# A mixture-of-experts kernel: experts visited in four groups ahead of the tail, 40 visits instead of 48

## The chip, the cores and the metric

The kernel runs on one core of a Trainium2 chip. Its engines are TensorE (PE in the profile, its weight loads PEld), VectorE (DVE), ScalarE (ACT), GpSimd (POOL) and SyncE (SP, which here only issues DMAs). The metric is the device time of one execution in microseconds; less is better.

## The reference, cut to what matters

A causal convolution of 7 taps with softmaxed weights per head runs over x (8 x 2880 rows of 192). Its 23,040 output rows go through a two-level mixture of experts: the best of 4 groups, then the best of that group's 4 experts, one expert of 16 for each row.

```python
g_idx = np.argmax(x @ w_group, axis=1)
# for each group g, of its rows xg:
e_idx = np.argmax(xg @ w_expert[g], axis=1)
h = np.maximum(xg[mask_e] @ w1[g, e], 0.0)      # 192 -> 1024
ye = h @ w2[g, e]                               # 1024 -> 192
out[tok_idx] = combined[:, None] * ye           # combined: both softmax weights
```

The results are float32. With the inputs used, the experts get between 1252 and 1628 rows.

## The kernel before

**Routing.** The rows are cut into 18 units of 4, 8 or 12 blocks of 120 rows; the last twelve units have 12 blocks. A unit (`unit`) convolves its rows on TensorE (line 498), ScalarE copies them to SBUF (lines 503, 505), and they are stored to the DRAM table `xcd` (lines 507, 664) with each row's softmax weight. Units 0 to 11 make their logits in float32 from TensorE transposes (lines 519 to 597). Units 12 to 17 (`THIN` = 12 and above) cut their rows into 16-bit parts on ScalarE and VectorE (`parts_a`, `parts_b`, lines 550 to 560), transpose these with DMAs issued by SP (`cross`, line 564) and multiply them on TensorE (line 573). VectorE then picks the expert and counts positions (lines 631 to 712), TensorE and VectorE make a list of row numbers for each expert (lines 718 to 722), and GpSimd scatters it into the table `idtab` (line 724).

**Where a unit's rows lie.** `rows_of` gives a unit a buffer from `room_tile`: by turns one of two `xc` tiles or one of two halves of the tile `spare`. Units 12 to 17 always take `xc`, since their 16-bit parts (`cut_tile`) lie in thirds of `spare`.

**Expert work.** It goes through `plan`, a list of slots. A slot gathers a block of row numbers (`gather`, GpSimd indirect DMA, line 806), transposes it on TensorE (`turn`, lines 824 to 830), multiplies by w1 (`hidden`, line 857; `hidden_wide`, line 895), applies relu (ScalarE, line 862) and forms the remainder `hl` (VectorE, line 863), multiplies by w2 (`back`, lines 875, 879), scales (ScalarE, line 933), adds (VectorE, line 940) and scatters into `out` (`finish`, line 941). To keep float32 accuracy on the fast matmul format every operand is split into a high and a low part. The first slot of an expert's turn is a visit: `weights` loads w1 and w2 through SP (lines 741 to 746) and ScalarE and VectorE split them in four steps (lines 763 to 776), into `ah`, `al`, `bb` and `cw`. Later slots of the same visit reuse the weights.

**The stages of the plan.** Portion 0 starts when 5 units are routed: one slot of 256 rows for each of the 16 experts. Portion 1 needs 12 units: two slots for each. The tail needs all units: the rest of each expert, in pieces. `PIECES` lists 16 sizes, from the largest rest to the smallest, such as (256, 384, 256); an expert's rank by its rest picks its entry, and `ORDER` the order in which ranks are visited. Visits: 16 + 16 + 16 = 48.

**What sets the order.** One program writes all queues. While it writes the slots it calls `advance` sixteen times a slot, which lets the units step forward at `rate`: the units' remaining stages until each portion's need, over the slots until that portion starts less 5 (`MARGIN`); the largest of these counts. `open_slot(i)` is called two slots ahead of slot i: it loads weights, and gathers. When the unit that a portion needs is finished, `open_portion` is called at most four `open_slot` calls later (`HOLD`): it reads the row numbers from `idtab` into `idp` through SP and moves each expert's consumed count `cons` on (`consume`). A scheduler then orders each engine's instructions.

```python
rate[0] = max(
    [(stages_to(portions[q][0]) - done[0]) / (max(starts[q] - MARGIN - i, 1) * 2 * NF)
     for q in starts if q not in idps] + [0.0])
```

## Time and profile before

| | |
|---|---|
| three timed runs, us | 1108.94, 1109.41, 1112.72; median 1109.41 |
| the profiled execution | 1113.36 us, span of its instructions 1111.6 us |
| TensorE matmul busy | 1060.5 us, 95% |
| weight loads on TensorE | 1030.6 us, 93% |
| VectorE | 776.5 us, 70% |
| ScalarE | 685.1 us, 62% |
| GpSimd | 538.2 us, 48% |
| DMA | 161.15 MB, mean 145 GB/s |
| mean granted clock of TensorE | 0.979 |

The span runs from the first to the last instruction; the profiled execution is 1.8 us longer than its span. Busy shares are means over very different stages: the first 92 us hold routing alone, the expert slots with routing beside them go on to about 530 us, and then slots run alone. So the windows by stage tell more than the page. Matmuls overlap in the records, and their ends are modelled. An arrow in a row names what ended an engine's idle time, which stands behind it in us.

### The profile page before, as it was taken

The numbers are of one execution on the slowest core, as the hardware profiler recorded it, in microseconds if no ns is written. First come the engines' busy times: TensorE is split into PE (matmuls) and PEld (weight loads), VectorE is DVE, ScalarE is ACT, GpSimd is POOL, SyncE is SP. The second block draws the span as 40 slices with busy tenths as digits, with TensorE's granted clock in tenths as the row PEclk, the third lists the DMA queues.
The fourth block names the chain that finished last, engine by engine and source line by source line (L and its number), as shares of the span: only waits on it lengthen the run. The fifth ranks groups of instructions, "written<-read, shape, count | busy, mean of one in ns | idle before, by whom it ended". The sixth has DMA issues, their size and how long they took to land. (4 is left out here: it accounts for less than half of the span.)

```text
span 1111.6 us, 22636 instructions
## 1 busy us (share of the span) xinstructions
PE 1060.5 (95%) x7986; PEld 1030.6 (93%) x7986; DVE 776.5 (70%) x1815; ACT 685.1 (62%) x1512; POOL 538.2 (48%) x485
## 2 busy tenths in 40 slices
PE   6799999989898999999999999999999999999997
PEld 5778899978898999999999999999999999999997
DVE  3746977788897888798669666656665656665662
ACT  5555566667674767675656666666666655655653
POOL 2013423334555555555646565555645555565542
PEclk9987999989999999999999999999999999999999
DMA  8978668898999777694455453333332323343210
GB/s 205 242 188 229 171 184 212 201 235 201 250 226 201 176 194 165 162 206 121 131 110 143 105 158 92 105 94 96 90 102 66 97 77 105 115 120 100 62 38 23
DMA packets 205814, 161.15 MB, mean 145 GB/s; under 512 B 87183, under 2 KB 189590, under 8 KB 205694
## 3 DMA queue, kind: packets, MB, share of 16 engines
q1 hardware_dynamic: 139696, 105.50, 37.6%
q0 software_dynamic: 19360, 36.09, 12.2%
q10 hardware_dynamic: 46638, 18.07, 7.5%
q8 instruction: 63, 1.03, 0.4%
q14 instruction: 57, 0.47, 0.2%
HBM read 113.06 MB, written 36.47 MB: 135 GB/s over the span
## 5 line engine op out<-in xcount | busy, mean ns | idle before, releaser
L875 PE MATMUL po<-cw,hh 128*128 128x384 f32 x1040 | 325.7, 371 | 1.1 <-ACT ys L933 1.1
L857 PE MATMUL ph<-xa,ah 128*128 128x256 f32 x1040 | 290.7, 300 | 6.8 <-DVE hl L863 3.3
L862 ACT ACTIVATE hh<-ph 128x512 fp32r<-128x512 f32 x260 | 153.6, 596 | 191.7 <-PE ph L857 145.9
L879 PE MATMUL po<-cw,hl 128*128 128x192 f32 x1040 | 261.8, 252 | 0.0
L863 DVE SCALAR_TENSOR_TENSOR hl<-ph,hh 128x512 fp32r<-128x512 f32 x260 | 176.9, 686 | 103.0 <-ACT hh L862 85.2
L806 POOL DMA_INDIRECT xg<-xcd,idp x128 | 149.1, 1165 | 195.3 <-ACT ys L933 115.2
L806 POOL DMA_INDIRECT xg<-xcd,idpt x127 | 135.4, 1066 | 162.9 <-ACT ys L933 67.1
L857 PE MATMUL ph<-xb,bb 128*128 128x256 f32 x1040 | 211.3, 285 | 1.8 <-DVE bb L768 1.8
L857 PEld LDWEIGHTS ph<-xa,ah 128*128 128x128 f32 x1040 | 199.9, 192 | 11.6 <-DVE hl L863 5.0
L879 PEld LDWEIGHTS po<-cw,hl 128*128 128x128 f32 x1040 | 200.2, 193 | 1.7
L875 PEld LDWEIGHTS po<-cw,hh 128*128 128x128 f32 x1040 | 197.3, 190 | 3.5 <-ACT ys L933 1.7
L857 PEld LDWEIGHTS ph<-xb,bb 128*128 128x128 f32 x1040 | 163.6, 193 | 2.2 <-DVE bb L768 2.0
L857 PE MATMUL ph<-xa,al 128*128 128x256 f32 x520 | 149.4, 287 | 0.0
L941 POOL DMA_INDIRECT out<-ys,idp x96 | 124.8, 1300 | 46.5 <-DVE ys L940 19.5
L941 POOL DMA_INDIRECT out<-ys,idpt x91 | 103.7, 1140 | 54.3 <-DVE ys L940 23.2
L933 ACT ACTIVATE ys<-po,xg 128x384 f32<-128x384 f32 x168 | 93.4, 580 | 34.8 <-PE po L879 14.9
L895 PE MATMUL ph<-xa,ah 128*128 128x384 f32 (+1 forms) x304 | 100.7, 335 | 4.2 <-DVE xc L901 3.3
L857 PEld LDWEIGHTS ph<-xa,al 128*128 128x128 f32 x520 | 100.3, 193 | 2.4 <-issue 0.2
L776 DVE TENSOR_TENSOR cw<-raw,cw 128x768 fp32r<-128x768 f32 x96 | 91.5, 953 | 9.9 <-ACT cw L775 7.0
L840 ACT ACTIVATE xb<-pm 64x128 fp32r<-64x128 f32 (+2 forms) x342 | 94.8, 277 | 3.1
L940 DVE TENSOR_TENSOR ys<-ys 128x192 f32<-128x192 f32 x179 | 61.7, 357 | 31.3 <-ACT ys L933 24.8
L775 ACT ACTIVATE cw<-raw 128x768 fp32r<-128x768 f32 x96 | 80.5, 845 | 0.1
(259 smaller groups left out, 2003.7 us busy)
## 6 DMA issues: line engine op xcount, KB each, us to landing
raw<-in_moe_w SPq DMA_DIRECT2D x96, 384.0 KB
raw<-in_moe_w SPq DMA_DIRECT2D x48, 512.0 KB
raw<-in_moe_w SPq DMA_DIRECT2D x48, 256.0 KB
xin<-in_x SPq DMA_DIRECT2D x7, 1134.0 KB
xcd<-xc ACTq DMA_DIRECT2D x10, 742.5 KB
xin<-in_x SPq DMA_DIRECT2D x6, 1039.5 KB
xcd<-xcb ACTq DMA_DIRECT2D x13, 360.0 KB
xcd<-spare ACTq DMA_DIRECT2D x3, 742.5 KB
```

The lines of the kernel that those rows point to most:

```text
L775: pin(PINW, nc.scalar.activation(out=cw[:, fs, 0, :], in_=rc[k - 2], func=AF.Copy))
L776: eng.get(k, nc.vector).tensor_tensor(out=cw[:, fs, 1, :], in0=rc[k - 2], in1=cw[:, fs, 0, :].bitcast(F32), op=ALU.subtract,)
L806: ins = nc.gpsimd.indirect_dma_start(out=rows[0:n, to:to + size], out_offset=None, in_=xcd[0:known, :], in_offset=bass.IndirectOffsetOnAxi ...
L840: nc.scalar.activation(out=xb[h:h + D2, 0, c:c + k], in_=pb, func=AF.Copy)
L857: nc.tensor.matmul(out=hp[:, j], lhsT=wgt[:, fs], rhs=xx, start=i == 0, stop=i == len(ops) - 1)
L862: nc.scalar.activation(out=hh, in_=hp, func=AF.Relu)
L863: lows.append(nc.vector.scalar_tensor_tensor(out=hl, in0=hp, scalar=0.0, in1=hh.bitcast(F32), op0=ALU.max, op1=ALU.subtract,))
L875: nc.tensor.matmul(out=oo[t][:, 0:2 * D], lhsT=hh[:, j, ts], rhs=cw[:, f].rearrange("p a d -> p (a d)"), start=f == 0, stop=False,)
L879: nc.tensor.matmul(out=oo[t][:, 0:D], lhsT=hl[:, j, ts], rhs=cw[:, f, 0, :], start=False, stop=f == NF - 1,)
L895: nc.tensor.matmul(out=hp[:, 0:w], lhsT=wgt[:, fs], rhs=xx, start=i == 0, stop=i == len(ops) - 1)
L933: nc.scalar.activation(out=y, in_=oo[t][0:n, 0:2 * D], func=AF.Copy, scale=g)
L941: nc.gpsimd.indirect_dma_start(out=outviews[nscat[0] % len(outviews)], out_offset=bass.IndirectOffsetOnAxis(ap=ids[t].bitcast(U32), axis=0 ...
```

## The change

The three stages before the tail become five entries of `portions`, each with a range of experts: experts 0 to 7 get one slot each when 5 units are routed; experts 8 to 11 two slots each at 9 units; experts 12 to 15 three slots each at 12 units; experts 0 to 7 two more slots each at 13 units. Visits: 8 + 4 + 4 + 8 + 16 = 40. Experts 8 to 11 thus have taken 512 rows before the tail instead of 768, so `PIECES` grows by 1024 rows in sum, with a new `ORDER`. `open_portion` and `consume` work on a range of experts. Besides, `rows_of` gives units 9, 10 and 11 the tile `xc` too (`THIN - 3`), and the last unit waits 16 stages instead of 8 before it makes its list (`list_lag`).

```diff
--- before.py
+++ after.py
@@ -77,12 +77,12 @@
     LE = P // E
     XT = 64
     PIECES = (
-        [(256, 384, 256)] * 2 + [(256, 320, 256)] * 2 + [(384, 384)] + [(384, 320)] * 4 + [(384, 256)] * 3
-        + [(320, 256)] * 2 + [(256, 256)] * 2)
+        [(256, 384, 256)] * 3 + [(256, 320, 256)] * 3 + [(384, 384)] * 3 + [(384, 320)] * 4 + [(384, 256)] * 2
+        + [(320, 256)])
     CAPS = [sum(p) for p in PIECES]
-    MOST, WMAX = CAPS[0], max(w for p in PIECES for w in p)
+    MOST, WMAX = -(-CAPS[0] // P) * P, max(w for p in PIECES for w in p)
     NTAIL = len(PIECES)
-    ORDER = [5, 0, 6, 2, 7, 3, 8, 1, 4, 14, 9, 10, 11, 12, 13, 15]
+    ORDER = [9, 0, 10, 1, 11, 2, 12, 3, 6, 4, 7, 5, 8, 13, 14, 15]
     assert NTAIL == E and sorted(ORDER) == list(range(E)) and sorted(CAPS, reverse=True) == CAPS
     CAP = -(-(N + MOST) // 1024) * 1024
     DUMMY = E * CAP
@@ -102,7 +102,7 @@
 
     NEED = 5
     NEXT = 6
-    portions = [(NEED, 1), (NU - NEXT, 2), (NU, 0)]
+    portions = [(NEED, 0, 8, 1), (9, 8, 12, 2), (12, 12, E, 3), (13, 0, 8, 2), (NU, 0, E, 0)]
     LEAD = 8
     LAG = 3
     REST = 10
@@ -280,7 +280,7 @@
     def rows_of(u):
 
         if u not in packed:
-            xc = room_tile(0 if u >= THIN else None)
+            xc = room_tile(0 if u >= THIN - 3 else None)
             xb = pa4.tile([P, UB, D2], F32, name="xcb")
             off = 0
             for v in range(u, NEED):
@@ -304,7 +304,7 @@
     make_identity(nc, ident)
 
 
-    LIM = SLOT * sum(spe for _, spe in portions)
+    LIM = SLOT * max(sum(spe for _, lo, hi, spe in portions if lo <= e < hi) for e in range(E))
     FR = 2 * E
     fill = wraw.tile([P, F], F32, name="raw")[0:FR, 0:LIM // 2].bitcast(I32)
     nc.gpsimd.memset(fill, BIG)
@@ -467,6 +467,10 @@
         ga, gl, gb, _ = gaps(u)
         nq = units[u][1] // QB
         return 1 + APART * (nq - 1) + 4 + CROSS + 1 + gb if u >= THIN else ga + gl + gb + 3 * nq
+
+    def list_lag(u):
+
+        return 2 * LISTLAG if u == NU - 1 else LISTLAG
 
     def unit(u, pre=None):
         c0, nb = units[u]
@@ -711,7 +715,7 @@
         with nc.allow_low_precision(reason="whole numbers, summed in float32"):
             nc.vector.tensor_reduce(out=rowi, in_=rows, axis=AX.X, op=ALU.add)
         counted[0] = u + 1
-        for _ in range(LISTLAG if u >= NEED else LISTLAG0 if u < NEED - 1 else 0):
+        for _ in range(list_lag(u) if u >= NEED else LISTLAG0 if u < NEED - 1 else 0):
             yield
         pl = bank("l")
         for b in range(nb):
@@ -1093,13 +1097,14 @@
         yield tabt
 
 
-    def consume(quota):
+    def consume(quota, lo, hi):
         nc.vector.scalar_tensor_tensor(
-            out=cons, in0=cons, scalar=float(quota), in1=eold[:, counted[0], 0:E], op0=ALU.add, op1=ALU.min,
+            out=cons[:, lo:hi], in0=cons[:, lo:hi], scalar=float(quota), in1=eold[:, counted[0], lo:hi],
+            op0=ALU.add, op1=ALU.min,
         )
 
     def stages(u):
-        return 1 + 8 + turning(u) + gaps(u)[3] + 1 + (LISTLAG if u >= NEED else 0)
+        return 1 + 8 + turning(u) + gaps(u)[3] + 1 + (list_lag(u) if u >= NEED else 0)
 
     SKEW1 = 8
     LIVE1 = 4
@@ -1116,7 +1121,8 @@
     live = []
     done = [0]
     routed = [0, 0]
-    needs = {need: pi for pi, (need, _) in enumerate(portions)}
+    needs = {need: pi for pi, (need, _, _, _) in enumerate(portions)}
+    assert len(needs) == len(portions)
 
     def step():
 
@@ -1175,28 +1181,29 @@
             yield
 
     def open_portion(pi):
-        need, spe = portions[pi]
+        need, lo, hi, spe = portions[pi]
         rows = spe * 2
-        idp = rows and const.tile([P, E, rows], I32, name=f"idp{pi}")
+        idp = rows and const.tile([P, hi - lo, rows], I32, name=f"idp{pi}")
         if pi == 0:
             pin(PINI, IQ.dma_start(
                 out=idp,
-                in_=idtab[0:E * CAP].rearrange("(e r) c -> e r c", e=E)[:, 0:P * rows, :].rearrange(
+                in_=idtab[0:E * CAP].rearrange("(e r) c -> e r c", e=E)[lo:hi, 0:P * rows, :].rearrange(
                     "e (p r) c -> p e (r c)", r=rows),
             ))
         elif rows:
-            ci = const.tile([1, E], I32, name=f"ci{pi}")
-            nc.vector.tensor_copy(out=ci, in_=cons[0:1])
+            ci = const.tile([1, hi - lo], I32, name=f"ci{pi}")
+            nc.vector.tensor_copy(out=ci, in_=cons[0:1, lo:hi])
             _, base = nc.values_load_multi_w_load_instructions(
                 ci, engines=[ET.SP], min_val=0, max_val=DUMMY - P * rows, skip_runtime_bounds_check_because=OOB_WHY,
             )
-            for e in range(E):
+            for e in range(hi - lo):
                 nc.sync.dma_start(
                     out=idp[:, e],
                     in_=idtab[bass.ds(base[e], P * rows), :].rearrange("(p r) c -> p (r c)", r=rows),
                 )
         idps[pi] = idp
-        consume(spe * SLOT)
+        if spe:
+            consume(spe * SLOT, lo, hi)
         if pi + 1 == len(portions):
             late.append(open_tail())
 
@@ -1226,7 +1233,7 @@
         w = pieces[k]
         return [(full + t, P) for t in range(w // P)] + [(part, XT)] * (w % P // XT)
 
-    plan = [(pi, e, s) for pi, (_, spe) in enumerate(portions) for e in range(E) for s in range(spe)]
+    plan = [(pi, e, s) for pi, (_, lo, hi, spe) in enumerate(portions) for e in range(lo, hi) for s in range(spe)]
     plan += [("tail", j, k) for j in ORDER for k in range(len(PIECES[j]))]
     weights_at = {}
     for i, (pi, e, s) in enumerate(plan):
@@ -1266,7 +1273,7 @@
             known = N
         else:
             W = pre.pop(e if pi == 0 else None, None) or weights(e * D, e * F, PENG(pi, e), held=pi == 0 and e > 1) if s == 0 else opened[i - 1][0]
-            ids = [idps[pi][:, e, k:k + 1] for k in (2 * s, 2 * s + 1)]
+            ids = [idps[pi][:, e - portions[pi][1], k:k + 1] for k in (2 * s, 2 * s + 1)]
             known = sum(n for _, n in units[:portions[pi][0]]) * BT
         opened[i] = (W, ids)
         gathered[i] = gather(ids, known, width(i), i >= E)
```

Lines in the new file lie 4 further down behind `list_lag`, so `hl` stands at line 867 and the weight loads at 745 to 750.

VectorE, in slot 1, counted from its input transposes to those of slot 2. Of before, its first rows; `al` and `bb` are steps of the weight split, all others but `hl` are routing:

```order
L863 SCALAR_TENSOR_TENSOR hl<-ph,hh 128x512 x3
L654 TENSOR_REDUCE ss<-dd 120x60
L656 TENSOR_TENSOR pick<-ss,oh 120x48
L863 SCALAR_TENSOR_TENSOR hl<-ph,hh 128x512
L657 TENSOR_REDUCE se<-pick 120x12
L658 TENSOR_SCALAR sg<-ss 120x12
L764 TENSOR_TENSOR al<-raw,ah 128x1024
L659 SCALAR_TENSOR_TENSOR se<-se,sg 120x12
L768 TENSOR_TENSOR bb<-raw,bb 64x1024
L863 SCALAR_TENSOR_TENSOR hl<-ph,hh 128x512
L721 TENSOR_SCALAR none<-pm 128x32
L660 RECIPROCAL spare<-se 120x12x4
```

Of after, rows of the same slot, ahead of its fourth `hl`; the others are routing:

```order
L663 SCALAR_TENSOR_TENSOR se<-se,sg 120x12
L713 TENSOR_TENSOR eold<-pm,eold 128x16
L647 TENSOR_TENSOR ohx<-oh 120x192
L664 RECIPROCAL xc<-se 120x12x4
L653 SCALAR_TENSOR_TENSOR cum<-keep_205,ohx 120x192
L686 TENSOR_REDUCE posn<-pos 120x12
L716 TENSOR_REDUCE rowi<-rows 128x1
L714 TENSOR_TENSOR rows<-eold,sel 128x17
L687 TENSOR_SCALAR posi<-posn 120x12
L689 TENSOR_SCALAR posi<-posn 120x12
L716 TENSOR_REDUCE rowi<-rows 128x1
L867 SCALAR_TENSOR_TENSOR hl<-ph,hh 128x512
```

Ahead of the first of these rows stand eleven more routing instructions, back to the `hl` before: 22 between two `hl`, where before there were at most three and two steps of the split.

SP's queue, where the first 16-bit unit's transposing DMAs (`ta<-spare`) stand among the loads of weights (`raw`). Of before:

```order
L741 DMA raw<-in_moe_w 128x1024
L252 DMA xin<-in_x 120x192
L254 DMA xin<-in_x 126x11x192
L742 DMA raw<-in_moe_w 64x1024
L564 DMA_TRANSPOSE ta<-spare 128x18x128 x2
L746 DMA raw<-in_moe_w 128x4x192
L564 DMA_TRANSPOSE ta<-spare 128x18x128
L746 DMA raw<-in_moe_w 128x4x192
L741 DMA raw<-in_moe_w 128x1024
L742 DMA raw<-in_moe_w 64x1024
```

Of after:

```order
L745 DMA raw<-in_moe_w 128x1024
L746 DMA raw<-in_moe_w 64x1024
L750 DMA raw<-in_moe_w 128x4x192 x2
L252 DMA xin<-in_x 120x192
L254 DMA xin<-in_x 126x11x192
L568 DMA_TRANSPOSE ta<-spare 128x18x128 x3
L745 DMA raw<-in_moe_w 128x1024
L746 DMA raw<-in_moe_w 64x1024
L750 DMA raw<-in_moe_w 128x4x192 x2
```

The three transposing DMAs stand together now, between the loads of one visit and those of the next; before, the two w2 loads (`128x4x192`) of a visit stood between and behind them.

## Rows read from the trace of the kernel before

**Rows 1.** The page, busy time of each engine, share, instructions

```profile
PE 1060.5 (95%) x7986; PEld 1030.6 (93%) x7986; DVE 776.5 (70%) x1815; ACT 685.1 (62%) x1512; POOL 538.2 (48%) x485
```

**Rows 2.** Windows by stage; columns as the first row names them

```profile
core 0: us, PE busy (x) PEld busy (x) DVE busy (x) ACT busy (x) POOL busy (x), PEclk, DMA share, GB/s
0.00:92.50 92.50, 73.37 (x525) 64.77 (x525) 51.95 (x233) 49.96 (x144) 16.75 (x35) 0.94 0.86 216
92.50:225.50 133.00, 128.26 (x982) 121.86 (x983) 101.26 (x249) 79.19 (x166) 43.95 (x38) 0.94 0.77 197
225.50:375.60 150.10, 135.69 (x1083) 129.55 (x1082) 128.69 (x257) 97.13 (x197) 73.78 (x55) 0.94 0.95 212
375.60:529.30 153.70, 152.50 (x1306) 149.12 (x1304) 131.47 (x285) 102.00 (x224) 88.15 (x73) 1.00 0.75 175
665.50:1111.60 446.10, 434.98 (x3048) 429.99 (x3046) 265.39 (x577) 268.97 (x604) 234.16 (x213) 1.00 0.30 87
```

**Rows 3.** Windows, one slot of 256 rows alone

```profile
548.88:558.53 9.65, 9.65 (x77) 9.65 (x76) 6.12 (x11) 6.67 (x13) 5.24 (x6) 1.00 0.34 84
```

**Rows 4.** TensorE's groups, logit matmuls, 225.5 to 375.6, then 375.6 to 529.3

```profile
L573 PE MATMUL pm<-wq,ta 128*128 128x60 bf16 x144 | 6.8, 191 | 3.4 <-DVE lsi L722 2.3 <-issue 1.2
L573 PE MATMUL pm<-wq,ta 128*128 128x60 bf16 x144 | 6.8, 190 | 0.5 <-issue 0.4
```

**Rows 5.** Windows, slots 9, 11 and 14

```profile
225.50:245.70 20.20, 14.80 (x129) 13.71 (x127) 20.08 (x40) 13.13 (x25) 9.12 (x5) 0.83 1.19 213
258.10:273.60 15.50, 13.55 (x86) 12.75 (x85) 10.88 (x23) 9.98 (x23) 4.54 (x4) 0.89 0.89 219
295.60:312.20 16.60, 14.34 (x137) 13.90 (x136) 12.97 (x23) 10.49 (x17) 9.24 (x7) 0.90 1.01 279
```

**Rows 6.** Timeline of VectorE and ScalarE, 218 to 227

```profile
224.62 1.90 DVE L554 TENSOR_TENSOR spare<-xc 128x512 f32<-128x512 f32 x3 [3.45 <-DMA xcd<-spare]
224.58 0.63 ACT L550 ACTIVATE spare<-xc 128x512 bf16<-128x512 bf16 x1 [3.58 <-DMA xcd<-spare]
```

**Rows 7.** Timeline of ScalarE, 225.5 to 375.6, waits for weights

```profile
263.70 0.60 ACT L862 ACTIVATE hh<-ph 128x512 fp32r<-128x512 f32 x1 [5.49 <-DMA raw<-in_moe_w]
297.88 1.06 ACT L763 ACTIVATE ah<-raw 128x1024 fp32r<-128x1024 f32 x1 [7.93 <-DMA raw<-in_moe_w]
```

**Rows 8.** VectorE's groups, weight splits, 225.5 to 375.6; last row 375.6 to 529.3

```profile
L776 DVE TENSOR_TENSOR cw<-raw,cw 128x768 fp32r<-128x768 f32 x21 | 20.0, 950 | 1.2 <-ACT cw L775 0.7 <-PE pm L498 0.4
L764 DVE TENSOR_TENSOR al<-raw,ah 128x1024 fp32r<-128x1024 f32 x10 | 12.1, 1214 | 6.0 <-ACT ah L763 6.0
L764 DVE TENSOR_TENSOR al<-raw,ah 128x1024 fp32r<-128x1024 f32 x7 | 8.6, 1225 | 3.0 <-ACT ah L763 2.0 <-issue 0.8
```

**Rows 9.** Windows, one piece of 384 and one of 256 rows

```profile
979.47:1003.85 24.38, 24.29 (x171) 23.97 (x170) 15.01 (x28) 15.35 (x33) 14.18 (x12) 1.00 0.36 104
```

**Rows 10.** Windows, slots 16 to 19

```profile
324.90:375.60 50.70, 47.01 (x383) 45.05 (x382) 41.15 (x88) 30.07 (x68) 24.23 (x21) 0.97 0.84 191
```

**Rows 11.** Windows, slots 0 and 1, 2 and 3, 4 to 8

```profile
92.50:112.80 20.30, 18.75 (x118) 17.74 (x119) 13.44 (x34) 9.08 (x20) 4.24 (x4) 0.69 0.75 203
112.80:144.00 31.20, 28.49 (x231) 27.25 (x230) 29.15 (x81) 17.70 (x32) 13.96 (x11) 0.95 0.65 176
144.00:225.50 81.50, 81.02 (x637) 76.87 (x636) 58.66 (x136) 52.41 (x115) 25.75 (x23) 1.00 0.82 204
```

**Rows 12.** Waits of GpSimd; timeline of SP from 79.7

```profile
POOL xg L806 <- DMA idp<-idtab: 7.3, 1, 7.3
80.28 2.76 SPq L254 DMA_DIRECT2D xin<-in_x  x1
```

**Rows 13.** Timeline of SP, 227 to 246

```profile
229.11 9.02 SPq L564 DMA_TRANSPOSE ta<-spare  x2
```

## The prediction

> **What bounds the kernel now.** I read the page's busy times first. TensorE is busy 95% of the span, VectorE 70%, ScalarE 62% [rows 1]. TensorE is in order, so the question is where its other 5% and its low clock lie. The windows by stage answer that [rows 2]; their edges are the starts of slots (a slot is the matmul work on one block of up to 384 gathered rows; its input transposes mark its start). Slots 0 to 8 run from 92.5 to 225.5 us, slots 9 to 19 to 375.6, slots 20 to 33 to 529.3, the tail's 36 slots from 665.5 to the end. TensorE's idle time in these four is 4.7, 14.4, 1.2 and 11.1 us, and 19.1 us before slot 0. The granted clock averages 0.94 up to the end of slot 19 and 1.00 afterwards.
>
> A slot of 256 rows with nothing beside it takes TensorE 9.65 us, busy throughout [rows 3]. Slots 9 to 19 are eleven such slots, 106.2 us, in 150.1 us: 43.9 us over. Slots 20 to 33 are fourteen, 135.1 us, in 153.7: 18.6 us over. Both hold the same routing work on TensorE, three units by their 144 logit matmuls [rows 4]. So 43.9 - 18.6 = 25.3 us of slots 9 to 19 is loss. The windows say nearly the same another way: 14.4 us idle plus 6% of 150.1 for the clock (9.0) is 23.4 [rows 2]. I use 23.4.
>
> What the loss consists of: the worst slots are 9, 11 and 14, where TensorE is idle 5.4, 1.95 and 2.3 us and the clock averages 0.83, 0.89 and 0.90 [rows 5]. In slot 9 VectorE is busy 20.08 of 20.20 us. Just before, VectorE and ScalarE both sat still for 3.5 us on the first 16-bit parts: the buffer `spare` that these write was still being stored as rows of an earlier unit (releaser: the DMA xcd<-spare) [rows 6]. Slots 11 to 14 also hold ScalarE's 7.9 and 5.5 us waits for expert weights [rows 7], with DMA engines busy 0.89 to 1.01 of their time [rows 5]. In this stretch every slot is a visit: ten w1 splits in eleven slots; slots 20 to 33 have seven in fourteen [rows 8].
>
> **The change, part by part.** All sums are against the profiled execution, 1113.4 us (span 1111.6); the median of the runs shown is 1109.4, 4.0 lower, and I move the result by that.
>
> *Matmul work.* 48 slots of 256 become 44, 36 tail pieces become 38. By widths: 65, 11 and 8 pieces of 256, 384 and 320 rows become 59, 15 and 8. Total rows stay 23,424. One 384 and one 256 piece in the tail together take 24.38 us [rows 9], so 384 takes 14.73. Four more of these (58.9) against six fewer of 9.65 (57.9): **+1.0**, bounded by 0 and 2. TensorE's work is the same, so anything won must come out of the idle and clock loss above.
>
> *Visits.* A visit loads one expert's w1 and w2 (192 x 1024 each, float32: 1.5 MB) and splits them on VectorE in four steps, one of 1.21 and two of 0.95 us [rows 8] and that of `bb`, as long in elements as the first: 4.3 us. Eight fewer is 12 MB and 35 us of VectorE, but what counts is where. In the order after the change, slots 9 to 19 hold 5 w1 splits instead of 10 and 12 w2 halves instead of 21: 5 x 2.42 + 9 x 0.95 = 20.7 us less VectorE. They hold 130 routing instructions instead of 114; at the page's mean (776.5 us / 1815 = 0.43) that is +6.9. VectorE goes from 128.7 to about 115 us, under TensorE's need of 106.2 + 18.6 = 125, and half the weight traffic of the stretch goes (five visits of ten).
>
> *Rows of units 9 to 11 out of `spare`.* The 3.5 us wait of rows 6 goes. What is late next there is the buffer `xc`, two deep, in which a unit's rows wait for their store before the unit two later writes. Units 12 to 17 already live that way, and in slots 20 to 33 TensorE is idle only 1.2 us, so I cost it nothing; without that cover it would be the same 3.5 us per unit.
>
> *Slots 9 to 19 together.* Best case all 23.4 us goes, as in slots 20 to 33. Worst case: slots 16 to 19 already had one visit per two slots and still lost 3.7 us idle and 3% of clock, 5.2 in four slots [rows 10], which is 14 in eleven, a gain of 9.4. Those four still carry late weights (DMA 0.84), so I take the middle: **-16**.
>
> *Slots 20 to 33.* Here 1.2 us idle is all there is; routing now ends about five slots earlier: **-1**, bounds 0 and -1.2.
>
> *Slots 0 to 8.* The second portion is due at slot 8 instead of 16, and the pace aims five slots ahead of it, so all of units 6 to 8 is pushed into slots 0 to 2. Slot 1 carries 50 routing instructions on VectorE instead of 8; slots 0 to 3 carry 82 instead of 67, slots 4 to 8 68 instead of 80. At 0.43 us: +6.4, then -5.2. VectorE was the late engine in 112.8 to 144.0 (29.15 of 31.2 us) but not in 144.0 to 225.5 (58.66 of 81.5) [rows 11], so the first counts more than the second gives back: **+3**. From below: all present loss gone, 4.7 idle + 8.0 clock, -12.7. From above: the 42 extra instructions of slot 1, never given back, +18.
>
> *Table reads.* The first id load covers 8 experts instead of 16. GpSimd waited 7.3 us for it [rows 12], and TensorE meanwhile had routing to do. It now stands behind an input load which took 2.8 us to issue [rows 12]. Gain and loss are of a size: **0**, bounds -3 and +3. Sixteen id loads in one portion become 4 + 4 + 8; the doubled list lag of the last unit ends about fifteen slots before the tail. Both cost nothing: SP and the units have slots to spare there.
>
> Sum: +1 - 16 - 1 + 3 + 0 = -13: 1113.4 becomes 1100.4, the median 1109.4 becomes **1096.4**.
>
> The headroom can be read another way. In slots 9 to 19 the weight loads on TensorE are busy 129.55 of 150.1 us [rows 2]. The Trainium skill (Perfetto Trace Analysis, Identifying the Most-Contended Engine) says that TensorE's headroom is judged by weight-load busy share, not by matmul busy share, since matmuls are pipelined. By that rule the ceiling of this stretch is 20.5 us instead of 23.4, the middle of the bounds is 15, and the median would come out at 1097.4; the trace's own idle plus clock stays my measure.
>
> **The rivals.**
> *More comes back.* Slots 9 to 19 become like 20 to 33 (-23.4) and slots 0 to 8 lose half their present loss (-6): with +1 and -1, -29, 1080. For it: one cause, the visit in every slot, stands behind most waits. Against it: slots 16 to 19 lost 5.2 us after that cause had gone.
>
> *Little comes back.* The routing of the 16-bit units itself makes the loss, at 1.3 us a slot: -9.4, and slots 0 to 8 cost +6: -3.4 with the rest, 1106. For it: slots 16 to 19. Against it: slots 20 to 33 route the same way without loss.
>
> *Slower.* VectorE is in order; hl releases the PSUM buffer ph, of which there are three. In slot 1 twenty-two routing instructions now stand between two hl; TensorE runs dry behind them, its clock falls as it did at 92.5 to 112.8 (granted 0.69) [rows 11], and the ids of the third portion come late, since they are read only once slot 14 has begun. Price: +18 for slot 1, half of it again in clock (+6 as 31% of 20 us), -9.4 from slots 9 to 19: +15, 1124. It decides if the way to the start of slot 9 grows by more than the 17 us won later. Against it: slots 2 and 3 of before held 58 routing instructions, and TensorE was idle 2.7 us there [rows 11].
> The first part of this has a page behind it: the Trainium skill (TensorE: Matmul & The Clock Gate, Architectural detail) states that VectorE's queue is strictly first in, first out; by that rule 22 routing instructions delay an hl by their whole length, and the rows on VectorE's full slot 9 agree.
>
> *No change.* Fewer visits, but the transposing DMAs on SP still hold up the next weights: 9.0 us for two [rows 13], and w2 loads stood among them. In the new order w2 loads no longer stand between the three. If the loads behind were late by as much as before, slots 9 to 14 keep their loss: -4 there, +3, +1: 1109.
> The change could also fail to do what it says: if an expert's rest exceeded its tail piece, extra 256-row visits would run. Counting the reference's rows per expert, the rests fit, by one row in the tightest; no chance of note.
>
> **How the numbers follow.** Forecast 1096.4: 0.57, its own range 1087 to 1104. More: 0.14. Little: 0.13. No change: 0.07. Slower: 0.09. Within 0.5% of 1109.4 is 1103.9 to 1114.9, about what a measurement of this kernel can tell from no change. Faster: 0.56 of the forecast, 0.14, and 0.04 of "little": 0.74. Same: 0.01 + 0.09 + 0.06 = 0.16. Slower: 0.09 and 0.01 = 0.10. The range cuts half of "more" below 1084 (0.07) and above 1109 "slower" and a little (0.11): 1084 to 1109.
>
> **What would show it.** Right: windows over slots 9 to 19 with TensorE idle under 6 us and clock near 1.00, VectorE under 120, no xcd<-spare wait at line 558 or 554, no ScalarE wait over 3 us for weights; slot 9 starting within 5 us of 225.5. Wrong: TensorE waiting for hl for several us in slots 1 to 3, a half-clock stretch there longer than now, xg late at slot 16, or the end moving less than the start of slot 20 does.

## The result, and the profile after

After: 1094.35 us median of 4 runs (1093.68 to 1099.95); before, on the same chip: 1110.1 (1108.94 to 1112.72). The ratio is 0.9868, 95% interval 0.9836 to 0.9900: faster, by 1.3%. Run again later, the pair gave 1098.24 against 1110.35, ratio 0.9891 (0.9859 to 0.9922). The forecast was 1096.4. Its sum and its stages are two things, and the stages came out less well than the sum.

The execution that the profile shows took 1099.95 us (span 1098.2), the longest of the four. The page's busy times, against [rows 1]:

```profile
PE 1053.3 (96%) x7908; PEld 1027.1 (94%) x7908; DVE 748.8 (68%) x1790; ACT 666.8 (61%) x1486; POOL 525.4 (48%) x483
```

TensorE is busy 7.2 us less in a span that is 13.4 us shorter; VectorE loses 27.7 us net: the splits of eight visits are 34.9 us (208.6 to 173.7), and other work grew by 7.2. Where the span went is read in the windows, cut at the same slots as [rows 2]: to slot 0, slots 0 to 8, 9 to 19, 20 to 33, and the tail.

```profile
core 0: us, PE busy (x) PEld busy (x) DVE busy (x) ACT busy (x) POOL busy (x), PEclk, DMA share, GB/s
0.00:101.80 101.80, 74.02 (x525) 65.16 (x525) 53.93 (x239) 50.21 (x144) 17.88 (x37) 0.91 0.87 218
101.80:237.50 135.70, 131.45 (x985) 124.83 (x985) 104.34 (x253) 84.69 (x174) 43.68 (x35) 0.92 0.73 181
237.50:367.60 130.10, 126.94 (x1088) 122.69 (x1088) 113.38 (x252) 82.23 (x175) 69.53 (x57) 1.00 0.98 211
367.60:519.80 152.20, 151.24 (x1301) 148.09 (x1300) 120.88 (x263) 95.10 (x209) 85.25 (x74) 1.00 0.60 145
616.30:1098.20 481.90, 473.12 (x3270) 469.82 (x3268) 285.23 (x619) 291.17 (x654) 249.86 (x231) 0.99 0.31 83
```

| stage | before us | after us | difference | predicted |
|---|---|---|---|---|
| start to slot 0 | 92.5 | 101.8 | +9.3 | 0 |
| slots 0 to 8 | 133.0 | 135.7 | +2.7 | +3 |
| slots 9 to 19 | 150.1 | 130.1 | -20.0 | -16 |
| slots 20 to 33 | 153.7 | 152.2 | -1.5 | -1 |
| the rest: slots from 34 on and the tail | 582.3 | 578.4 | -3.9 | +1 |
| span | 1111.6 | 1098.2 | -13.4 | -13 |

In slots 9 to 19 TensorE is idle 3.2 us (14.4 before), its clock 1.00 (0.94). The stretch still moves 211 GB/s (212 before) with the DMA engines' share at 0.98 (0.95). So a full share by itself is no loss. Before, TensorE's waits there named VectorE (10.2 us of the 14.4) and ScalarE (2.3), never a transfer; it was ScalarE that waited for transfers of weights [rows 7]. The longest of before (columns: who waited, for whom, us in total, times, longest):

```profile
PE ph L857 <- DVE hl L863: 2.7, 4, 1.4
PE pm L573 <- DVE lsi L722: 2.3, 1, 2.3
PE pm L498 <- ACT xc L503: 1.9, 1, 1.9
```

The largest now:

```profile
PE ph L861 <- DVE hl L867: 2.9, 3, 1.9
```

VectorE's splits in the stretch, against [rows 8]: 12 halves of w2 and 6 of the w1 operation, where there were 21 and 10.

```profile
L780 DVE TENSOR_TENSOR cw<-raw,cw 128x768 fp32r<-128x768 f32 x12 | 11.3, 956 | 0.8 <-ACT cw L779 0.7
L768 DVE TENSOR_TENSOR al<-raw,ah 128x1024 fp32r<-128x1024 f32 x6 | 7.3, 1225 | 1.2 <-ACT ah L767 1.2
```

The first slots and slot 9 alone, against [rows 5, 11]:

```profile
101.80:114.70 12.90, 11.85 (x66) 11.19 (x67) 6.53 (x23) 3.87 (x10) 1.96 (x2) 0.55 0.51 138
114.70:137.50 22.80, 21.17 (x165) 20.14 (x164) 19.63 (x64) 11.41 (x21) 8.22 (x6) 0.85 0.44 103
237.50:249.90 12.40, 11.81 (x128) 11.38 (x127) 12.27 (x31) 6.15 (x12) 8.18 (x6) 1.00 1.13 229
```

Slot 0 runs at a clock of 0.55 and slot 1 takes 22.8 us; slot 9, which took 20.2 us with VectorE full, takes 12.4. By the records of the granted clock TensorE runs at half speed (1.2 GHz) from 93.0 us on for 20.5 us (13.7 before). That is where TensorE goes idle ahead of slot 0; but before it fell too, at 91.6 us, with TensorE at work, so the idle time does not explain the fall itself, only perhaps its length. Timeline rows of SP, GpSimd and TensorE show that idle time, against [rows 12] (columns: start, us, engine, line, operation; in brackets the idle time before and its releaser):

```profile
69.45 10.49 SPq L254 DMA_DIRECT2D xin<-in_x  x2
82.03 0.39 SPq L1188 DMA_DIRECT2D idp<-idtab  x1
...
92.86 1.60 POOL L810 DMA_INDIRECT xg<-xcd,idp  x1 [14.28 <-DMA raw<-in_moe_w]
...
101.78 0.45 PE L828 MATMUL pm<-ident,xg 128*128 128x128 f32 x1 [8.77 <-DMA xg<-xcd,idp]
```

The first read of the id table (line 1188) is issued at 82.03, behind the input loads; GpSimd's first gather, which needs it, starts at 92.86, 10.8 us later (5.5 us in before: 79.79 to 85.30). The profile puts that wait down to a load of weights that landed last; before, it named the id read. TensorE stands still for 8.8 us until gathered rows arrive (0.4 us in before).

### The profile page after: what moved, and what is told of

Same layout as the page of the kernel before. It is cut to its first block, busy times and chain, and to the rows that moved or that the text cites. A ratio compares the mean times of both kernels' runs of the same rounds, so it can differ in the third digit from the quotient of the medians.

```text
span 1098.2 us, 22337 instructions
## 1 busy us (share of the span) xinstructions
PE 1053.3 (96%) x7908; PEld 1027.1 (94%) x7908; DVE 748.8 (68%) x1790; ACT 666.8 (61%) x1486; POOL 525.4 (48%) x483
## 4 chain that ended last, share of the span: by engine, by line
PE 79%; DMA 7%; DVE 6%; ACT 4%; issue 3%; POOL 1%; POOLq 0%; ACTq 0%; SPq 0%; DVEq 0%
PE ph L861 23%; PE po L879 14%; PE ph L899 12%; PE po L883 6%; PE po L917 6%; PE pm L502 3%; PE pm L917 3%; PE po L923 3%; DMA out<-ys,idpt 2%; PE pm L828 2%; DMA xg<-xcd,idp 1%; DMA xcd<-spare 1%; PE pm L597 1%; DMA idp<-idtab 1%; PE pm L923 1%
## 5 line engine op out<-in xcount | busy, mean ns | idle before, releaser
L879 PE MATMUL po<-cw,hh 128*128 128x384 f32 x944 | 295.0, 370 | 0.4 <-ACT ys L937 0.4
L861 PE MATMUL ph<-xa,ah 128*128 128x256 f32 x944 | 262.1, 298 | 7.5 <-DVE hl L867 4.1
L883 PE MATMUL po<-cw,hl 128*128 128x192 f32 x944 | 237.1, 251 | 0.0
L867 DVE SCALAR_TENSOR_TENSOR hl<-ph,hh 128x512 fp32r<-128x512 f32 x236 | 161.2, 688 | 110.4 <-ACT hh L866 109.0
L861 PE MATMUL ph<-xb,bb 128*128 128x256 f32 x944 | 192.3, 285 | 0.0
L861 PEld LDWEIGHTS ph<-xa,ah 128*128 128x128 f32 x944 | 181.5, 192 | 11.2 <-DVE hl L867 5.2
L883 PEld LDWEIGHTS po<-cw,hl 128*128 128x128 f32 x944 | 180.9, 192 | 1.5
L879 PEld LDWEIGHTS po<-cw,hh 128*128 128x128 f32 x944 | 178.3, 189 | 2.3 <-ACT ys L937 0.6
L945 POOL DMA_INDIRECT out<-ys,idp x88 | 111.5, 1267 | 35.7 <-issue 14.4
L899 PE MATMUL ph<-xa,ah 128*128 128x384 f32 (+1 forms) x368 | 122.1, 334 | 0.6 <-DVE spare L905 0.5
L899 PE MATMUL ph<-xb,bb 128*128 128x384 f32 (+1 forms) x368 | 90.1, 326 | 0.0
```

The lines of the kernel that those rows point to most:

```text
L861: nc.tensor.matmul(out=hp[:, j], lhsT=wgt[:, fs], rhs=xx, start=i == 0, stop=i == len(ops) - 1)
L867: lows.append(nc.vector.scalar_tensor_tensor(out=hl, in0=hp, scalar=0.0, in1=hh.bitcast(F32), op0=ALU.max, op1=ALU.subtract,))
L879: nc.tensor.matmul(out=oo[t][:, 0:2 * D], lhsT=hh[:, j, ts], rhs=cw[:, f].rearrange("p a d -> p (a d)"), start=f == 0, stop=False,)
L883: nc.tensor.matmul(out=oo[t][:, 0:D], lhsT=hl[:, j, ts], rhs=cw[:, f, 0, :], start=False, stop=f == NF - 1,)
L899: nc.tensor.matmul(out=hp[:, 0:w], lhsT=wgt[:, fs], rhs=xx, start=i == 0, stop=i == len(ops) - 1)
L945: nc.gpsimd.indirect_dma_start(out=outviews[nscat[0] % len(outviews)], out_offset=bass.IndirectOffsetOnAxis(ap=ids[t].bitcast(U32), axis=0 ...
```

## The experiments

Theory at the outset: the gain is in slots 9 to 19 and comes from fewer visits (splits and weights) and a little from the rows out of `spare`; the loss at the start comes from the place of the id read. The rivals are given with each run. The runs fell on three chips, on which the kernel before took 1114.9 (first to fourth experiment), 1110.35 (fifth to eighth) and 1107.1 us (ninth to twelfth). Times are compared on one chip; stages are read from one profiled execution each, those of before from the profile ahead of the change. How far such a reading can be trusted: the visits alone, one kernel on two chips, took 133.6 and 129.9 us for slots 9 to 19.

**1. The rows alone.** Before, with one edit:

```diff
-            xc = room_tile(0 if u >= THIN else None)
+            xc = room_tile(0 if u >= THIN - 3 else None)
```

> The kernel before with the one edit that takes the row pieces of units 9 to 11 out of the buffer `spare`; the visits are as before. Theory of the prediction: only the wait of 3.5 us on the copy to DRAM (rows 6) goes, and it fed the other waits of slot 9, so the time is 1110.1 - 3.5 = about 1106.6 (1102 to 1108), and slots 9 to 19 (150.1 us before) become about 146. Rival, the wait is hidden anyway or taken over by the next operation of VectorE: within 2 us of 1110.1, stretch 149 to 151. Second rival, the edit is most of the gain of the whole change: below 1100, stretch below 138.

1112.44 us, ratio 0.9991 (0.9963 to 1.0018): no change that can be measured. The wait on the copy is gone from VectorE and ScalarE, and the stretch is 148.2 us, 1.9 shorter; TensorE now waits elsewhere, for the transposing read of the 16-bit parts:

```profile
228.90:377.10 148.20, 132.46 (x1082) 126.16 (x1081) 125.09 (x251) 93.97 (x188) 72.59 (x55) 0.97 0.95 215
...
PE pm L573 <- DMA ta<-spare: 6.4, 1, 6.4
```

**2 and 7. The visits alone.** After, with the same edit undone; twice, since the first had no changed kernel beside it.

> The changed kernel with that one edit undone: the row pieces of units 9 to 11 are in `spare` again, the visits stay as after. Theory of the prediction: most of the gain comes from the visits, the waits on the copy come back (units 9 to 11 now come in other slots): 1094.4 + 3.5 = about 1098 (1096 to 1101), slots 9 to 19 about 133.5 instead of 130.1. Rival, the edit is worth nothing: 1093.5 to 1095.5. Second rival, the edit is most of the gain: above 1104, stretch above 142.

> The visits alone (the row pieces of units 9 to 11 in `spare` again), once more, to have it beside the whole change on one chip. Theory: the edit on the row pieces is worth what its wait was, 3 to 5 us (slots 0 to 8 were 140.0 us with the visits alone and 135.7 with both), so this run is 3 to 6 us over the changed kernel of this call. Rival: it is worth nothing, within 2 us. Second rival: over 8 us, most of the change's gain.

1111.48 us on the first chip (ratio 0.9967, 0.9941 to 0.9992) and 1098.69 on the second (0.9893, 0.9864 to 0.9922), where the whole change took 1098.24 (0.9891). So the visits carry the gain, and the rival of both texts (the edit is worth nothing) holds within what can be measured. How large the gain is depends on the chip: the same kernel won 0.3% on the first and 1.1% on the second, with intervals that don't overlap, and the runs don't show why. Locally the prediction's wait is real: it comes back, 2.8 us on ScalarE and 2.5 on VectorE, and slot 8 takes 15.6 instead of 12.5 us.

```profile
ACT spare L554 <- DMA xcd<-spare: 2.8, 1, 2.8
```

In the two profiles of the second chip slot 34 starts 3.3 us later with it (520.9 instead of 517.6). But the end moved by 0.5 us in the medians, of six executions each that spread over 4 and 7 us; in the profiles 1.8 us came back in the tail (480.3 instead of 482.1 us), where the changed kernel has a half-clock stretch of 3.4 us at 1079.8 and this one has none.

**3. The id read on GpSimd's queue.**

```diff
-    IQ = nc.sync
+    IQ = nc.gpsimd
```

> The changed kernel with the first read of the id table issued by GpSimd, right after GpSimd's own writes of the table, instead of by SP, where in the profile after it is issued at 82.03 us behind two input loads and lands 10.8 us later. Theory: the term 'table reads: 0' of the prediction failed because of the place in SP's queue; the read lands some 5 us after its issue as before, slot 0 begins at 93 to 97 us of the span instead of 101.8, and the time is 1088 to 1091. Rival, the read is slow because the input loads and weights occupy the DMA engines whatever queue it is in: slot 0 still at 100 to 103, time 1093 to 1096. Second rival, the start is made up for later by the rush of routing in slots 1 and 2: slot 0 is early, slot 9 still begins at 235 to 238, time as after.

1106.46 us, ratio 0.9928 (0.9907 to 0.995), with no changed kernel beside it on that chip. By the stages the first rival holds, nearly: slot 0 at 99.4, against 99.8 in the visits alone on the same chip, where SP issues the read. The read is issued at 82.20, and the gather still waits until 90.22:

```profile
82.20 0.95 POOL L1188 DMA_DIRECT2D idp<-idtab  x1 [3.03 <-DMA idtab<-lsi,rowi]
90.22 1.07 POOL L810 DMA_INDIRECT xg<-xcd,idp  x1 [7.07 <-DMA xin<-in_x]
```

Another queue doesn't move the bytes of the input load out of the way. The Trainium skill (DMA: Bandwidth & Descriptors, Issuing engines are not separate DMA queues) says that transfers started by the scalar, sync or gpsimd engine run on the same 16 DMA engines and interleave there; these 8.0 us, with the read in GpSimd's queue, agree.

**4. The rush spread out.**

```diff
-    MARGIN = 5
+    MARGIN = 3
```

> The changed kernel with MARGIN 3 instead of 5, so the planner gives the routing of units 5 to 8 two more slots before the second group of visits opens, and the routing instructions stand less densely between the operations of slots 1 and 2. Theory: the rush costs TensorE its waits there (slots 1 to 3 took 52.8 us in the profile after, 10 us over four slots' normal 9.65 plus routing), so they shorten by 2 to 5 us and the time is 1090 to 1092. Rival: the routing only moves to slots 3 to 5 and the stages are the same in number, time 1093 to 1096. Second rival: the second group's first visit at slot 8 gets its rows late, and TensorE waits there over 3 us: 1097 or more.

1118.66 us, ratio 1.004 (1.0008 to 1.0073): worse. Slots 0 and 1 took 24.1 us instead of 35.4 (fifth experiment), but slots 0 to 8 together 134.3, the same. MARGIN also sets the pace to the later groups and to the tail; there this kernel took 162.5 us for slots 20 to 33 (155.5 with the visits alone on the same chip) and 14.9 instead of 9.65 for the last slot ahead of the tail, though the latter holds gaps for which the profile names no releaser (last section). Windows: slots 0 and 1, 2 to 8, 20 to 33, and slot 43:

```profile
101.90:126.00 24.10, 22.70 (x156) 21.62 (x157) 13.99 (x36) 9.51 (x20) 1.80 (x2) 0.73 0.51 138
126.00:236.20 110.20, 104.99 (x813) 100.08 (x812) 85.38 (x199) 69.60 (x139) 40.43 (x33) 0.95 0.72 193
367.40:529.90 162.50, 155.67 (x1308) 150.86 (x1307) 129.97 (x285) 98.23 (x220) 90.28 (x74) 0.99 0.67 154
617.60:632.50 14.90, 11.09 (x77) 10.85 (x76) 6.89 (x12) 6.13 (x13) 8.98 (x9) 0.93 0.73 196
```

So in these profiles the rush is no net loss: the routing costs slots 0 to 8 about the same wherever in them it stands.

**5. The change again**, beside the others of its chip.

> The changed kernel as it is, to see it on the same chip as the other kernels of this call. The earlier call's kernels stood against a kernel before of 1114.9 us (1110.1 when the change was timed), and their stages 20 to 33 and the last part came out 3 us longer each than in the profile after, though their instructions there are the same. Theory: that is the chip or the hour, not their edits; here too the ratio to before is 0.990 to 0.995 and not 0.987, with waits of 0.6 to 2 us at the same slots (27, 63, 68, 72). Rival: the edits caused it; this run gives 0.984 to 0.989 and none of these waits.

1098.24 us, ratio 0.9891: between the two ranges. None of the small waits: slots 27, 63 and 68 took 12.0, 10.9 and 10.9 us as in the profile after, where the visits alone had 14.1, 11.9 and 11.5 on the first chip. The same visits-only kernel, run again on this one, hadn't them either. So these waits go with the chip or the hour, not with the edits. Its start is that of the profile after:

```profile
91.58 1.05 POOL L810 DMA_INDIRECT xg<-xcd,idp  x1 [12.77 <-DMA raw<-in_moe_w]
...
101.02 0.45 PE L828 MATMUL pm<-ident,xg 128*128 128x128 f32 x1 [7.94 <-DMA xg<-xcd,idp]
```

**6. The id read ahead of the input.** Two rows of SP's queue change places and nothing else:

```diff
-            pin(PINI, IQ.dma_start(
+            idread[0] = pin(PINI, IQ.dma_start(
...
-                    load_part(xin, off, v, hold=lambda ins: pin(0 < u <= PINL, ins))
+                    with tc.issue_after(idread[0].ins) if u == 9 else nullcontext(): load_part(xin, off, v, hold=lambda ins: pin(0 < u <= PINL, ins))
```

```
 L254 DMA xin<-in_x 126x11x192
-L254 DMA xin<-in_x 126x12x192
 L1188 DMA idp_1030<-idtab 128x8x2
+L254 DMA xin<-in_x 126x12x192
 L750 DMA raw<-in_moe_w 128x4x192
```

> The changed kernel with two rows of SP's queue swapped and nothing else: the first read of the id table now stands before the load of unit 9's input (1134 KB), as in the kernel before, instead of behind it. Theory: the 10 us between issue and landing come from sharing the DMA engines with that load, whichever queue issues the read (the read on GpSimd's queue took 8 us and won 2 us); with the load issued behind it the read lands in 5 to 6 us, the first gather starts at 85 to 87 us, slot 0 at 93 to 96 instead of about 100 to 102, and 5 to 7 us of the time go, unless slots 1 and 2 give it back. Rival: what the read waits for is GpSimd's writes of the table, so it is issued no earlier and lands no earlier: slot 0 at 99 to 102, time as after. Second rival: unit 9's input comes late and its routing with it, slot 9 or 12 waits: no gain in spite of an early slot 0.

1092.17 us (1088.12 to 1092.69) against 1098.24 (1094.48 to 1101.21): every run is below every run of the changed kernel, 6 us in the medians; ratio to before 0.9827 (0.9793 to 0.986). It is the best version found.

```profile
82.80 0.39 SPq L1188 DMA_DIRECT2D idp<-idtab  x1
83.30 0.94 SPq L254 DMA_DIRECT2D xin<-in_x  x1
...
89.59 1.05 POOL L810 DMA_INDIRECT xg<-xcd,idp  x1 [9.82 <-DMA idp<-idtab]
...
96.30 0.45 PE L828 MATMUL pm<-ident,xg 128*128 128x128 f32 x1 [2.23 <-DMA xg<-xcd,idp]
```

The read is issued no earlier (82.80 against 82.49), and the gather follows after 6.8 us instead of 9.1 (I had expected 5 to 6). The gathered rows come 6.7 us after that instead of 9.4, with the input behind them. TensorE waits 2.2 us instead of 7.9, and slot 0 starts at 96.3 instead of 101.0; the half-clock stretch is 10.2 us instead of 20.5. The read's 8 KB are slow even alone: in the row of the DMA engines' rate from 83.5 to 92 us (40 slices) some 2 us pass at 1 to 3 GB/s before the input load comes through.

```profile
GB/s 226 217 162 59 11 2 2 1 3 2 3 2 1 2 1 6 34 67 82 125 183 230 335 340 418 287 321 298 282 257 242 263 275 299 283 297 316 354 347 349
```

**8, 9, 10. Splits and loads taken from four visits.** Before, where visits 9, 11, 13 and 15 don't split (8), don't load (9), or do neither (10). The edit shown is the tenth's; the eighth lacks the changes to `raw` and to `range(2)`, the ninth those to `W["old"]` and `W["todo"]`:

```diff
-        raw = [wraw.tile([P, F], F32, name="raw") for _ in range(4)]
+        raw = old["raw"] if old else [wraw.tile([P, F], F32, name="raw") for _ in range(4)]
...
-            for k in range(2):
+            for k in range(0 if old else 2):
...
-        W["todo"] = [lambda k=k: split(k) for k in range(4)]
...
+                old=opened[i - 1][0] if pi == 0 and e in (9, 11, 13, 15) else None) if s == 0 else opened[i - 1][0]
...
+        if old:
+            W["old"] = old
+        W["todo"] = [] if old else [lambda k=k: split(k) for k in range(4)]
```

> The kernel before, where visits 9, 11, 13 and 15 of the first group still load their weights but don't split them, and compute with the split tiles of the visit before (their products are those of another expert). Theory: the split work on VectorE and ScalarE is what slots 9 to 19 lose; without four of the ten splits VectorE has 4 x (1.21 + 1.22 + 2 x 0.95) = 17 us less, the stretch falls from 150.1 (148.2 in the first experiment) by 10 to 16 us to 134 to 140. Rival, the weights' transfers are the cause (ScalarE waited 5.5 and 7.9 us for them): the loads are all still there, so the stretch stays within 4 us, 145 to 150.

> The kernel before, where visits 9, 11, 13 and 15 of the first group don't load their weights, and split the raw tiles of the visit before once more (their products are those of another expert). The split work is all there, 6 MB of transfers are not. Theory, formed after the split's removal left the stretch at 149.2 us: the transfers are the cause. The weights, the copies of rows to DRAM and the transposing reads share the DMA engines, whose mean busy share was 0.95 in slots 9 to 19; the stretch falls to 132 to 140 us, ScalarE's waits for weights go. Rival, neither alone: either one suffices to fill the stretch, so it stays at 146 to 150 here and falls only when both go. Second rival, it is the order of the routing (which unit falls where), and both experiments leave it: 146 to 150 here and in the run with neither.

> The kernel before, where the same four visits neither load nor split and compute with the tiles of the visit before (products of another expert). Theory, the transfers: as without the loads, within 3 us of it. Rival, either one suffices: 128 to 136 while the other two stay above 145. Second rival, the order of the routing: 145 or more.

1107.74 us without the splits (one run); 1100.42, ratio 0.9933 (0.9906 to 0.9959), without the loads; 1097.94, ratio 0.9908 (0.9878 to 0.9938), with neither. First the window over slots 9 to 19 without the splits, and two of ScalarE's waits in it:

```profile
225.60:374.80 149.20, 132.06 (x1083) 127.71 (x1082) 113.68 (x242) 86.05 (x182) 70.19 (x55) 0.95 0.92 206
...
ACT spare L550 <- DMA xcd<-spare: 8.2, 1, 8.2
ACT ah L763 <- DMA raw<-in_moe_w: 7.9, 1, 7.9
```

The same window without the loads:

```profile
233.40:372.00 138.60, 130.60 (x1083) 124.98 (x1082) 127.40 (x255) 96.25 (x195) 73.23 (x55) 0.98 0.85 192
```

With neither, slot 9 and then slots 9 to 19:

```profile
231.20:251.80 20.60, 14.69 (x129) 13.82 (x128) 18.00 (x41) 11.54 (x23) 8.90 (x5) 0.83 1.16 234
231.20:365.50 134.30, 128.39 (x1083) 124.61 (x1082) 113.04 (x241) 85.20 (x181) 69.73 (x55) 0.97 0.90 191
```

The stretch goes from 150.1 to 149.2, 138.6 and 134.3 us. The first theory (the splits) falls: VectorE lost 15 us of work and the stretch 0.9, while the waits for transfers stayed, 8.2 us for the copy out of `spare` and 7.9 for weights. Without the loads it lost 11.5, with neither 15.8. The loads are the larger cause; the splits read 0.9 alone and 4.3 after the loads, both near the scatter of one reading. Without the loads slots 0 to 8 took 138.0 us instead of 133.0, so part of the 11.5 is lost again ahead of the stretch; with neither they took 133.0. The whole times say 2.6 us for the splits (one run), 6.6 for the loads and 9.1 for both. The routing's order is that of before in all three, so it is not the cause of these gains.

One rival stands untested: a load that goes also leaves SP's queue, so these runs don't part the bytes in the DMA engines from the place in the queue. The trace of before shows that the place has a part. ScalarE's 7.9 us wait for weights [rows 7] began at 289.95, but the load that ended it was issued only at 293.0, right behind two transposing DMAs that held SP for 9.7 us:

```profile
283.18 9.72 SPq L564 DMA_TRANSPOSE ta<-spare  x2
293.00 0.53 SPq L741 DMA_DIRECT2D raw<-in_moe_w  x1
```

Slot 9 remains: 20.6 us with neither (first row of the last windows), VectorE busy 18.0 of them, with the routing that stands packed there.

**11, 12. Loads or splits added to the change.** After, where the later slots of a visit in slots 9 to 19 (six) load their weights again into tiles that nobody reads, or split the same raw tiles again:

```diff
-            W = pre.pop(e if pi == 0 else None, None) or weights(e * D, e * F, PENG(pi, e), held=pi == 0 and e > 1) if s == 0 else opened[i - 1][0]
+            W = weights(e * D, e * F, held=True, old=opened[i - 1][0]) if s and 8 < i < 20 else pre.pop(e if pi == 0 else None, None) or weights(e * D, e * F, PENG(pi, e), held=pi == 0 and e > 1) if s == 0 else opened[i - 1][0]
```

> The other way round: the changed kernel, where the second and third slots of a visit between slots 9 and 19 (six of them) load their expert's weights once more into raw tiles that nobody reads, so that the stretch has eleven visits' transfers and five visits' splits. The instructions of TensorE, VectorE and ScalarE stand in the order of the changed kernel. Theory, the transfers: slots 9 to 19 grow from 130.1 to 140 to 150 us, with waits on transfers (rows, transposes or weights) showing again. Rival, the splits: 129 to 133. Second rival, the order of the routing: 129 to 133 here, and likewise with the splits added.

> The changed kernel, where the same six slots split the raw tiles of their visit again into fresh tiles, without a load: eleven visits' splits, five visits' transfers, VectorE from 113 to about 135 us in the stretch. Theory, the transfers: VectorE is fuller than TensorE there, but the stretch grows by no more than 4 us, 130 to 134. Rival, the splits of the prediction's working: 138 to 150, TensorE waiting for hl. Second rival, the order of the routing: 129 to 133.

1124.38 us, ratio 1.0166 (1.0132 to 1.0201), with the loads; 1118.75, ratio 1.0104 (1.0074 to 1.0134), with the splits. Each is slower than before, and the changed kernel's gain (not measured on this chip) is gone with either. Slots 9 to 19 with the loads, with TensorE's longest waits and ScalarE's longest for transfers:

```profile
232.70:389.50 156.80, 134.44 (x1088) 129.06 (x1088) 114.07 (x252) 81.81 (x176) 69.35 (x57) 0.95 1.02 226
...
PE pm L577 <- DMA ta<-spare: 8.4, 2, 5.5
PE po L879 <- ACT ys L937: 6.8, 1, 6.8
...
ACT xc L507 <- DMA idp<-idtab: 10.1, 2, 5.6
ACT spare L556 <- DMA raw<-in_moe_w: 7.9, 1, 7.9
```

And with the splits:

```profile
235.00:379.10 144.10, 134.14 (x1088) 127.96 (x1087) 133.56 (x273) 99.31 (x198) 75.52 (x57) 0.96 0.86 180
...
PE ph L861 <- DVE hl L867: 5.2, 4, 2.6
```

The loads cost 26.7 us (130.1 to 156.8), more than expected, with VectorE's work as it was (114.1 us): TensorE waits 8.4 us for the transposed parts, ScalarE 7.9 for weights and 10.1 for what the profile names an id read. The splits cost 14.0 (144.1) and 7.0 more in slot 20, where TensorE waits for hl; I had expected 4 at most, so the theory "transfers alone" falls too. Both matter: 26.7 us for the loads, 21.0 for the splits with slot 20.

## Why the prediction was right, and where it wasn't

**Slots 9 to 19, -16 (measured -20.0).** Right in place, sign and bounds (-9.4 to -23.4); 4 us too small. Every mark that I named for it is there: idle 3.2 us, clock 1.00, VectorE 113.4 us (115 forecast), no wait on the copy, none of ScalarE for weights. Its working counted VectorE's microseconds and only named the weight traffic. The runs weigh them: four visits' loads 11.5, their splits 0.9 alone and 4.3 after the loads.

Two readings in it are off: not every slot of before's stretch is a visit (9 to 15, 16 and 18 are), and the changed stretch holds six w1 splits, not five. The run with neither holds six too, with 13 w2 halves against 12, so the 4.2 us between it and the change are no visits' worth; slot 9, whose routing now stands earlier, is 8.2 us shorter in the change (12.4 against 20.6). I did not try that apart.

"Little comes back" falls with the 20.0, and so does "no change": nothing waits for weights any more. "More comes back" falls in its second half, since slots 0 to 8 gained nothing. The Trainium skill's measure in the prediction (Perfetto Trace Analysis, Identifying the Most-Contended Engine: headroom by weight-load busy share) gave a ceiling of 20.5 us here; the stretch gave 20.0, and weight loads are now busy 122.7 of 130.1. The nearness is partly luck: 6.9 of the 20.0 us are weight loads that themselves take less time (129.6 to 122.7), which that ceiling leaves out, and 7.4 us without a weight load remain.

**The rows of units 9 to 11, 3.5 us within the -16.** The wait went, as named. Its worth at the end did not show: no change alone (0.9991, with an interval that reaches 4.1 us), and 0.5 us in company, where the profiles have 3.3 us up to slot 34. Whether it is worth anything at the end stays open.

**Table reads, 0 (measured +9.3): the step that failed.** "Gain and loss are of a size: 0, bounds -3 and +3." I saw that the read would stand behind an input load and priced this by the 2.8 us that the load took on SP. That row is the time of issuing. The Trainium skill (Perfetto Trace Analysis, Per-instruction lifecycle: what the profiler-reported window actually captures) says in general that for a DMA the whole data movement lies outside the reported window; the 0.39 us of the row at 82.03 beside the 10.8 agree.

The load's 1134 KB pass through the DMA engines afterwards, and the read shares them. In the DMA records of the trace the read's 1024 packets of 8 bytes run from 83.7 to 90.0 us, beside the load's; before, its 2048 ran from 81.0 to 83.8, ahead of the load's first at 84. From issue to gather it was 10.8 us where there were 5.5. The other runs agree: 5.1 to 6.8 us in the six kernels whose read stands ahead of that load, 9.1 to 10.8 in the seven where SP reads behind it.

I also took it that TensorE had routing to do meanwhile; it ran out at 93.0. Swapping the two rows brought back 6 us of the time. The 9.3 us are the largest of the pairs: on the other chips slot 0 began 2.0 to 8.5 us later in the changed kernels than in those built on before.

**Slots 0 to 8, +3 (measured +2.7; 134.3 in the fifth experiment, +1.3).** The size is right, the reason is doubtful: the spread rush left the stage at 134.3. VectorE's queue was not what decided, and the "slower" rival, built on that, had no ground: TensorE waited for no hl in slots 0 to 3, and the way to slot 9 grew by 12.0 us, not by the 17 from which that rival decides. The longer half-clock stretch, which I had listed as a sign against me, is there, but it starts at 93.0, ahead of slot 0; in slots 1 to 3 themselves half speed took 10.2 us, 10.8 before. Those 12.0 us are also outside my 5; 9.3 of them are the start.

**Slots 20 to 33, -1 (measured -1.5).** Right.

**Matmul work, +1 (measured -3.9 from slot 34 on).** The term was right, the pair of profiles misleads: from slot 34 to the end before took 582.3 us in its profiled execution, and 577.4 to 577.6 in the three kernels of the eighth to tenth experiment, which are the same there; the change took 578.4 and 578.7. On one chip the changed kernels are 0.6 us below to 1.3 above those built on before: about the +1. The profiled execution of before had about 4.8 us of its own in this part, 2.7 of them in TensorE's waits for VectorE's low halves (3.3 instead of 0.6); a row of the tail's waits in before, and in the ninth experiment:

```profile
PE ph L895 <- DVE xc L901: 3.3, 5, 1.8
```

```profile
PE ph L896 <- DVE xc L902: 0.6, 3, 0.2
```

So the sum of -13 was right by luck, by errors of opposite sign: +9.3 at the start against -4.0 in slots 9 to 19 and -4.9 that was the profiled run's own.

## What to carry to other kernels

A small read that gates the start (ids, indices, a table) is priced by when its bytes and those of its consumer get through the DMA engines, not by its issue row: look for the large load just ahead of it in any queue, and put it behind. Where DMA engines and a vector engine are both nearly full, either can be the cause: take away each alone and both, add each back, and read the whole times beside the stage. Here the stage read 0.9 and 11.5 alone and 15.8 together, the whole times 2.6, 6.6 and 9.1, which sum. And before a term is read off the difference of two profiled executions, look at the stages that the change can't have touched: they give the run's own error, here 5 us of 13.

## What the runs showed of the hardware

The DMA engines' share of 0.95 to 0.98 and the rate of 211 to 212 GB/s in slots 9 to 19 were the same with 14.4 us of TensorE idle and with 3.2; with the added loads they were 1.02 and 226. In these stretches the share did not tell whether anyone waits.

Reading the ids took 5.1 to 6.4 us from issue to the gather that needs them for the 16 KB of before and the kernels built on it, and 6.8 us for 8 KB in the sixth experiment, though the transfers beside it had nearly stopped. In the DMA records the 2048 packets of 8 bytes of before pass in 2.8 us, the 1024 of the sixth experiment in 4.3. Its size was not what it cost.

On the chip of the first four experiments, TensorE had gaps of 0.2 to 1.2 us between matmuls for which the profile names no releaser (in slot 27 of the visits alone, and in slot 43 with the spread rush, four of 0.6 to 1.2 us that left TensorE busy 11.1 of 14.9 us). The visits alone had none in slot 27 on the second chip, and slot 43 took 9.6 and 9.7 us in the visits alone and in the kernel of the third experiment on the first; the spread rush ran on that chip only. What makes these gaps stays open. Such a row, in the slot 43 named:

```profile
627.60 0.34 PE L879 MATMUL po<-cw,hh 128*128 128x384 f32 x1 [1.17 <-issue]
```
